# Four sums for the seven-for-eight products: from two engines to one

## The chip, the cores and the metric

One core of a Trainium2 chip runs the kernel. The metric is the device time of one execution in microseconds, the median of several runs.

## The reference

```python
X = np.fft.fft(x, axis=1)                    # x: 8 batches, 3008 rows, 256 columns, float32
X = np.fft.fft(X, axis=2)
x2 = X.real.reshape(24064, 256)
h = x2 @ w_in                                # 256 -> 2048
g = h * (1.0 / (1.0 + np.exp(-1.702 * h)))   # the GELU with a sigmoid
out = g @ w_out                              # 2048 -> 256
```

## The kernel before

The Fourier transforms are matrix products with tables. The rows of a batch are folded first (sums and differences of mirrored columns and rows, `fold1`), then mixed by TensorE (`mix1`, stage one), sent through DRAM (`spill`, `fill`) and mixed again (`stage2`). The column transform is folded into the first weight matrix (`wcs`), so the hidden layer is made straight from stage two's output `pq`.

The second half is a list of 384 steps, `steps`: eight batches, each of three blocks, two halves and eight pairs of hidden chunks, so that a batch has 48 steps. A step `t` makes two chunks of the hidden layer for up to 256 rows and for the mirrored 256 rows. The words "place p" mean the step's number within its batch, `t` modulo 48. Eight steps are a group: they add up in PSUM to one piece of the output.

The output product of two chunks is a product of 2 x 2 blocks. From step 8 on it is done in the manner of Strassen and Winograd, with seven products of blocks in place of eight. That needs four sums of the hidden blocks: S1 = A21 + A22, S2 = S1 - A11, S3 = A11 - A21 and S4 = A12 - S2. For all but the last group (`deep`) three of the products are themselves divided in this way, which needs four more sums for each pair of steps (`deeper`). All blocks stand in one SBUF tile, `big`: A11, A21, S3, S2 of four steps in the part LEFT, and A12, S4, A22, S1 of six steps in the part RIGHT.

The order on every engine is the order in which the code is written (a manual schedule); the engines meet only at semaphores. One iteration `t` of the loop over steps does, for TensorE, the hidden product of step t and the start of step t+1 (`begin`), the output products of step t-3 (`product`, LAG is 3) and the small products of the steps before. For the other engines it does this:

- ACT: `forward(t)`, the GELU of the forward half (L607, from PSUM tile `x` into `big`); `doubled(t+1)`, twice the hidden value (L604, tile `g`); `activate_back(t)`, the GELU of the mirrored half (L614); `middle(t+2)`, which writes the middle term into the PSUM bank of step t+2 (L592). That bank is the one that step t has used, so it must have been read by then. TensorE adds the hidden product of step t+2 to it.
- VectorE: `backward(t)`, which makes the mirrored half from `g` and `x` (L565; it reads the PSUM bank of step t for the last time); then S2 and S4 for a pair of steps (L629, L630; 512 columns in one operation, in every second iteration); then `deeper`, three operations in one iteration and one in the next (L651).
- GpSimd: S1 and S3 of step t (L622 and L623, 256 columns each, in every step), right after `activate_back(t)`.

At the end of a group VectorE also combines the result (`combine`: L757, L758; `combine_small`: L786; `combine_last`: L768, L804) and transposes it (`turn_last`: L737), and around stage two it transposes the new `pq` (L371). In two groups of each batch the second half has 226 rows only; for those `combine` has GpSimd clear a strip of the output buffer (the memset, L752).

Side work is hung on the iterations by `at(t, ...)`, after everything else of the iteration. For the batch after the present one these are, with t0 the first step of the present batch:

```python
for c in range(NCH):                          # 8
    for part in range(2):
        at(t0 + 6 + 2 * c + part + late, fold1, b + 1, c, part, nc.gpsimd)
    if c % 2:
        k = t0 + 9 + 2 * c + late + (c == (5 if late else 1))
        at(k, mix1, b + 1, c // 2)
...
            for k in range(4):
                at(t0 + 31 + 2 * k + late, paced, t0 + 31 + 2 * k + late)
                at(t0 + 31 + 2 * k + late, load_x, b + 2, k)
```

`late` is 5 in the first batch and 0 in the others. So half a fold stands in each of 16 iterations, from place 6 to place 21, in GpSimd's queue between the sums of one step and those of the next: L218 to L220 once for the edge tile `e`, and then for each c L225 and L227 (part 0), L230 and L231 (part 1). All of them read and write SBUF. The rows that they fold were loaded in the batch before, by `load_x` at places 31 to 37 (36 to 42 in the first batch); its DMAs are issued by SP, and a tiny DMA ahead of each (`paced`) holds SP's queue until ACT has reached that step. A fold waits for the load; `mix1` waits for the folds.

Of the kernel before, what the change touches and what calls it, by code (L numbers as in the profile page):

```python
# [29 lines left out]
ALU = mybir.AluOpType  # L30
# [20 lines left out]
def free(ap, offset, *dims):  # L51
    return bass.AP(ap.tensor, ap.offset + offset, [list(ap.ap[0])] + [list(d) for d in dims])
# [60 lines left out]
def kernel(ctx: ExitStack, tc, x, w_in, w_out, tab1, tab2, out):  # L113
    nc = tc.nc
# [12 lines left out]
    op = ctx.enter_context(tc.tile_pool(name="op", bufs=2, space=SB))  # L127
# [25 lines left out]
    big = cv.tile([128, 19 * 1024], F32, tag="big", name="big")  # L153
# [220 lines left out]
    def nyquist(b, blk):  # L374

        nb = nbt[b, blk] = pqp.tile([128, 512], F32, tag="nb", name="nb")
        row = pqt[b, blk][0:1, 1, :]
        if (b, blk) != (0, 0):
            nc.sync.dma_start(out=nb[:], in_=view(Nd, (b * NBLK + blk) * 512, [0, 128], [1, 512]))
            return  # L380
        ps = bank("psn")
        halves(ps[:], ones[:], row, start=True, stop=True)
        nc.scalar.copy(nb[:], ps[:])
# [29 lines left out]
    def squares(key, eng, lo=0, n=1024):  # L413
        g, hi = pre[key][0][:, lo:lo + n], raw[key][:, lo:lo + n, 1].bitcast(F32)
        if eng is nc.scalar:
            eng.activation(g[:], hi, ACTF.Square)
        else:
            eng.tensor_tensor(g[:], hi, hi, op=ALU.mult)
# [5 lines left out]
    def low_up(key, lo=0, n=1024):  # L424

        nc.scalar.activation(pre[key][2][:, lo:lo + n].bitcast(F32), raw[key][:, lo:lo + n, 0], ACTF.Copy, scale=2.0 ** -29,
                             bias=2.0 ** 23)
# [76 lines left out]
    def no_row(c0):  # L504
        nc.sync.dma_start(out=wcs[1][0:1, c0:c0 + 1024], in_=tab1[127:128, n0 + 4:n0 + 1028])

    NP = NF // 2
    steps = [(b, blk, hh, p) for b in range(B) for blk in range(NBLK) for hh in range(2) for p in range(NP)]
    vb, ht, xb, gt, pot = {}, {}, {}, {}, {}
    LEFT, MADE, RIGHT, SUM, RES, OUT = 0, 4096, 8192, 14336, 16384, 18432  # L510
    A11, A21, S3, S2 = range(4)
    A12, S4, A22, S1 = range(4)
# [3 lines left out]
    def width(t):  # L516

        return 226 if steps[t][1:3] == (0, 1) else 256
# [9 lines left out]
    def hidden(t):  # L528

        n = width(t)  # L530
        pa, pb = (bank(name, f"b{i}" if t == NP - 3 else None) for i, name in enumerate(("pa", "pb")))
        for ps, cs in ((pa, 0), (pb, 1)):
            for i in range(2):
                halves(ps[:, i * 256:i * 256 + n], *operands(t, cs, i), start=(i == 0), stop=(i == 1))
        v = sp.tile([128, 512], F32, tag="v", name="v")
        nc.scalar.copy(two(v[:], n), two(pa[:], n))
        vb[t] = v, pa, pb

    def at_left(t, q):
        return LEFT + t % 4 * 1024 + q * 256  # L540

    def at_right(t, q):
        return RIGHT + (t // 2 % 3 * 2 + t % 2) * 1024 + q * 256

    def left(t, q, n):
        return big[:, at_left(t, q):at_left(t, q) + n]

    def right(t, q, n):
        return big[:, at_right(t, q):at_right(t, q) + n]
# [35 lines left out]
    def middle(t):  # L585

        b, blk, hh, p = steps[t]
        n = width(t)
        x = xb[t] = bank("x", f"b{t % 2}")
        for i in range(2):  # L590
            f = 2 * p + i
            nc.scalar.activation(x[:, i * 256:i * 256 + n], nbt[b, blk][:, hh * 256:hh * 256 + n], ACTF.Copy,  # L592
                                 scale=af1[:, f:f + 1])

    def begin(t, cs=0):

        n = width(t)
        for i in range(2):
            halves(xb[t][:, i * 256:i * 256 + n], *operands(t, cs, i), start=False, stop=(cs == 1))
# [13 lines left out]
    def activate_back(t):  # L613
        nc.scalar.activation(back(t), back(t), ACTF.Gelu_apprx_sigmoid)  # L614

    def sums(t, eng):

        if not NP <= t < len(steps):
            return
        n = width(t)  # L620
        if eng is nc.gpsimd:
            eng.tensor_tensor(right(t, S1, n), left(t, A21, n), right(t, A22, n), op=ALU.add)  # L622
            eng.tensor_tensor(left(t, S3, n), left(t, A11, n), left(t, A21, n), op=ALU.subtract)  # L623
            return
        if t % 2 == 0:
            return
        a11, s2 = (free(big[:], at_left(t - 1, q), [1024, 2], [1, n]) for q in (A11, S2))
        a12, s4, s1 = (free(big[:], at_right(t - 1, q), [1024, 2], [1, n]) for q in (A12, S4, S1))
        eng.tensor_tensor(s2, s1, a11, op=ALU.subtract)  # L629
        eng.tensor_tensor(s4, a12, s2, op=ALU.subtract)  # L630

    def deep(t):

        return NP <= t < last
# [301 lines left out]
    n = len(steps)  # L936
# [21 lines left out]
    for b in range(B):  # L958
        t0 = b * NBLK * NF
        late = 0 if b else 5  # L960
# [28 lines left out]
    for t in range(n + LAG):  # L989
        if t < NP:  # L990
            if t == NP - 3:
                spare[:] = [tag for tag in spare if tag[0] == "o"] + ["b2"]
            if t == NP - 1:
                middle(NP)
            hidden(t)
            if t == NP - 1:
                begin(NP)
                no_row(1024)
            if t == 0:
                squares(in2, nc.scalar)  # L1000
                nyquist(0, 0)
                low_up(in2)
                low_down(in2)
            if t in rows_at:
                first_row(rows_at[t])
            if t >= LAG and t != LAG + 1:
                product(t - LAG, 0, None)
            if t == LAG:
                product(1, 0, None)
            if t == 5:  # L1010
                bounds(("out", 2))
            if t == 6:
                low_down(("out", 3))
            if t:
                activate(t - 1)
            if t == 3:
                bounds(("in", 3))
            if t == 5:
                bounds(("out", 3), False)
            if t in early:  # L1020
                fold_w(early[t])
            rows(t)
            if t == NP - 1:
                doubled(NP)
                middle(NP + 1)
        else:
            after, special = (any(fn in (mix1, stage2) for fn, _ in extra.get(k, ())) for k in (t - 1, t))
            if t < n:
                begin(t, 1)
            if t == NP:  # L1030
                activate(t - 1)
            if after and t + 1 < n:
                middle(t + 1)
            if t < n:
                forward(t)
            while waiting:
                m, ps = waiting.pop()
                mixed(m, 1, ps)
            opening = (t - LAG) % NP == 0 and t >= NP + LAG
            one, other = (t - LAG, (1, 2, 4, 7)), (t - LAG - 1, (5, 6, 3))  # L1040
            if opening:
                small_products(*other)
            cut = 0 if opening and not after else 3 if after else 2
            product(t - LAG, 0, cut)
            if after:
                small_products(one[0], one[1][:1])
                small_products(other[0], () if opening else other[1][:1])
            if t + 1 < n:
                begin(t + 1)
            if not opening:  # L1050
                small_products(other[0], other[1][after:])
            product(t - LAG, cut, 6 if t - LAG == last else None)
            small_products(one[0], one[1][after:])
            swap(t - LAG - 2)
            if t < n:
                backward(t)
            if t + 1 < n:
                doubled(t + 1)
            if t < n:
                activate_back(t)  # L1060
                sums(t, nc.gpsimd)
            if t + 2 < n and not special:
                middle(t + 2)
            combine_small(t - LAG - 1)
            if t - LAG == last:
                product(last, 6, None)
            sums(t - 1, nc.vector)
            deeper(t - 2, 0)
            deeper(t - 3, 1)
        if t == NP:  # L1070
            psu.close()
            low = ctx.enter_context(tc.tile_pool(name="low", bufs=1, space=PS))
            pot["low"] = low.tile([128, 3 * 512], F32, tag="low", name="low")
        if t >= LAG:
            combine(t - LAG)
            combine_last(t - LAG - 2)
            turn_last(t - LAG - 3, 0)
            turn_last(t - LAG - 4, 1)
        if t >= NP:
            spare[:] = [f"b{t % 2}"] * special + ["b2"]  # L1080
        for fn, args in extra.get(t, ()):
            fn(*args)
# [28 lines left out]
```

## Time and profile before

| what | value |
|---|---|
| median of 3 runs | 1856.31 us (1854.34 to 1856.57) |
| span of the profiled execution, first to last instruction | 1853.1 us |
| TensorE busy | 1836.6 us |
| VectorE busy | 1520.9 us |
| ACT busy | 1150.5 us |
| GpSimd busy | 975.2 us |
| granted TensorE clock | 0.999 of full speed |

The profiled execution is recorded by its span alone; what lies around it is taken as the difference to the median, 3.2 us. The engines are named PE (TensorE's products), PEld (its weight loads), DVE (VectorE), ACT (ScalarE), POOL (GpSimd) and SP (SyncE, which issues DMAs here). In the timeline a row has its start, its duration, the engine, the line of the kernel, the operation, the tile written and those read, the shapes, how many were merged into the row, and in brackets the idle time before it with what ended it. In a table of waits a row has the total in us, how often, and the longest. In a table of windows a row has the stretch, its length, then for PE, PEld, DVE, ACT and POOL the busy time (and the number of instructions), the granted clock, the share of the DMA engines and GB/s.

### The profile page before, as it was taken

To read this page: it belongs to the slowest core of one execution; us is meant where nothing else is said; L and a number is where in the kernel's file an instruction comes from. 1 tells how busy PE (TensorE), PEld (TensorE's weight loads), DVE (VectorE), ACT (ScalarE), POOL (GpSimd) and SP (SyncE) were. 2 spreads that over 40 slices of the span, in tenths; PEclk is the share of its full clock that TensorE was granted. 3 is DMA by queue.
4 is the path that set the end of the run, shared out by engine and by line. 5 is a ranking of instruction groups with operands and counts; after the bars stand their busy time and mean duration, and the time that the engine had idled before them with its cause. 6 is when DMAs were issued, how large, how long until landed. Compare 5 with 4: busy or idle time off the path is not lost.

```text
span 1853.1 us, 56093 instructions
## 1 busy us (share of the span) xinstructions
PE 1836.6 (99%) x23722; PEld 1401.3 (76%) x23722; DVE 1520.9 (82%) x2222; ACT 1150.5 (62%) x2241; POOL 975.2 (53%) x1053
## 2 busy tenths in 40 slices
PE   8999999999999999999999999999999999999998
PEld 4677777777777777777777777777777777778776
DVE  6988778887798778987789878888888888878874
ACT  5666656665666666666566666666665666656663
POOL 4776446744368434773348643485445754444442
PEclk9999999999999999999999999999999999999999
DMA  8721340215012240223302132121411111100111
GB/s 280 181 61 34 85 67 19 72 52 99 19 46 48 73 81 13 52 50 90 57 13 67 43 86 52 19 75 35 103 31 23 37 46 36 31 19 13 23 19 24
DMA packets 149707, 105.31 MB, mean 57 GB/s; under 512 B 106057, under 2 KB 130665, under 8 KB 148896
## 3 DMA queue, kind: packets, MB, share of 16 engines
q1 hardware_dynamic: 146624, 99.68, 23.6%
q8 instruction: 187, 3.06, 0.7%
q10 hardware_dynamic: 2832, 2.05, 0.5%
q14 instruction: 64, 0.52, 0.1%
HBM read 64.41 MB, written 48.05 MB: 61 GB/s over the span
## 4 chain that ended last, share of the span: by engine, by line
PE 80%; DVE 9%; POOL 4%; ACT 2%; DMA 2%; issue 2%; SPq 0%; DVEq 0%; ACTq 0%; POOLq 0%
PE x L184 29%; PE o L184 22%; PE low L685 21%; PE o L685 3%; DVE big L651 3%; PE ps L255 2%; DVE big L786 2%; DVE big L565 1%; PE ps L365 1%; POOL xt L227 1%; DVE big L629 1%; POOL big L623 1%; DMA xt<-in_x_dram 1%; ACT big L607 1%; DMA Td<-big 1%
## 5 line engine op out<-in xcount | busy, mean ns | idle before, releaser
L622 POOL TENSOR_TENSOR big<-big 128x256 f32<-128x256 f32 (+1 forms) x376 | 353.0, 939 | 825.1 <-ACT big L614 691.4
L184 PE MATMUL x<-pq,wcs 128*64 128x256 f32 (+1 forms) x6016 | 768.8, 376 | 2.0 <-ACT g L604 1.4
L651 DVE TENSOR_TENSOR big<-big 128x512 f32<-128x512 f32 (+1 forms) x736 | 623.1, 861 | 23.4 <-PE low L685 4.7
L184 PE MATMUL o<-big,wo 128*64 128x256 f32 (+1 forms) x4800 | 620.8, 375 | 0.1
L184 PEld LDWEIGHTS x<-pq,wcs 128*64 128x64 f32 x6016 | 412.3, 137 | 186.0 <-issue 15.0
L184 PEld LDWEIGHTS o<-big,wo 128*64 128x64 f32 x4800 | 341.6, 137 | 148.0 <-DVE big L629 0.5
L604 ACT ACTIVATE g<-x 128x512 f32<-128x512 f32 (+1 forms) x376 | 221.6, 589 | 366.3 <-PE x L184 365.0
L565 DVE TENSOR_TENSOR big<-g,x 128x512 f32<-128x512 f32 (+2 forms) x440 | 254.1, 589 | 209.4 <-ACT big L607 209.0
L592 ACT ACTIVATE x<-nb,af 128x256 f32<-128x256 f32 (+1 forms) x752 | 352.9, 469 | 79.7 <-DVE pq L371 63.6
L685 PE MATMUL low<-big 128*64 128x128 f32 (+1 forms) x5888 | 382.8, 270 | 0.0
L685 PEld LDWEIGHTS low<-big 128*64 128x64 f32 x5888 | 337.5, 137 | 29.2
L623 POOL TENSOR_TENSOR big<-big 128x256 f32<-128x256 f32 (+1 forms) x376 | 352.6, 938 | 0.0
L607 ACT ACTIVATE big<-x 128x512 f32<-128x512 f32 (+1 forms) x376 | 219.2, 583 | 127.5 <-PE x L184 121.3
L614 ACT ACTIVATE big<-big 128x512 f32<-128x512 f32 (+1 forms) x376 | 231.9, 617 | 46.0 <-DVE big L565 44.0
L685 PE MATMUL low<-big,wo 128*64 128x128 f32 (+1 forms) x2944 | 220.4, 271 | 0.1
L685 PEld LDWEIGHTS low<-big,wo 128*64 128x64 f32 x2944 | 171.3, 137 | 4.2 <-DVE big L651 1.4
L630 DVE TENSOR_TENSOR big<-big 128x512 f32<-128x512 f32 (+1 forms) x188 | 160.8, 855 | 6.5
L629 DVE TENSOR_TENSOR big<-big 128x512 f32<-128x512 f32 (+1 forms) x188 | 137.3, 730 | 5.3 <-POOL big L622 5.3
L786 DVE TENSOR_TENSOR big<-big,low 128x512 f32<-128x512 f32 (+3 forms) x184 | 109.0, 609 | 3.5
L685 PEld LDWEIGHTS o<-big,wo 128*64 128x64 f32 x1472 | 92.2, 137 | 25.0
L685 PE MATMUL o<-big,wo 128*64 128x128 f32 (+1 forms) x1472 | 110.0, 270 | 0.0
L227 POOL TENSOR_TENSOR xt<-xt 111x510 f32<-111x510 f32 x56 | 86.0, 1535 | 4.4
(95 smaller groups left out, 966.2 us busy)
## 6 DMA issues: line engine op xcount, KB each, us to landing
out_dram<-os SPq DMA_DIRECT2D x284, 64.0 KB
t<-Td SPq DMA_DIRECT2D x22, 512.0 KB
Td<-xt SPq DMA_DIRECT2D x56, 192.0 KB
xt<-in_x_dram SPq DMA_DIRECT2D x14, 512.0 KB
xt<-Xr SPq DMA_DIRECT2D x14, 512.0 KB
nb<-Nd SPq DMA_DIRECT2D x23, 256.0 KB
out_dram<-os SPq DMA_DIRECT2D x96, 56.0 KB
Xr<-in_x_dram SPq DMA_DIRECT2D x7, 752.0 KB
```

The costliest lines, as they stand in the source:

```text
L184: nc.tensor.matmul(out[c0:c0 + 64], lhsT=lhs[:, c0:c0 + 64], rhs=rhs, skip_group_check=True, **how)
L565: nc.vector.tensor_tensor(free(out, at + m - 1, [by, 2], [RUN, blocks], [-1, m]), *ins, op=op)
L592: nc.scalar.activation(x[:, i * 256:i * 256 + n], nbt[b, blk][:, hh * 256:hh * 256 + n], ACTF.Copy, scale=af1[:, f:f + 1])
L604: nc.scalar.activation(two(g[:], n), two(xb[t][:], n), ACTF.Copy, scale=2.0)
L607: nc.scalar.activation(front(t), two(xb[t][:], width(t)), ACTF.Gelu_apprx_sigmoid)
L614: nc.scalar.activation(back(t), back(t), ACTF.Gelu_apprx_sigmoid)
L622: eng.tensor_tensor(right(t, S1, n), left(t, A21, n), right(t, A22, n), op=ALU.add)
L623: eng.tensor_tensor(left(t, S3, n), left(t, A11, n), left(t, A21, n), op=ALU.subtract)
L629: eng.tensor_tensor(s2, s1, a11, op=ALU.subtract)
L630: eng.tensor_tensor(s4, a12, s2, op=ALU.subtract)
L651: nc.vector.tensor_tensor(out, i0, i1, op=how)
L685: nc.tensor.matmul(o, lhsT=lhs, rhs=rhs, start=first_in, stop=(p == NP - 2), skip_group_check=True)
```

## The change

S1 and S3 leave GpSimd. VectorE makes them like S2, for two steps in one operation of 512 columns: in every second iteration it does S1, S3 and S2 of the pair that the two iterations before have finished, in this order. S4 is made one iteration later than the others (in the last group, which needs it sooner, in the same one), ahead of the next three sums of `deeper`. GpSimd keeps, in the loop over steps, the folds of x and the memset. The place of the folds in the code is the same.

```diff
-    def sums(t, eng):
-
-        if not NP <= t < len(steps):
+    def sums(t, part):
+
+        if not NP <= t < len(steps) or t % 2 == 0:
             return
         n = width(t)
-        if eng is nc.gpsimd:
-            eng.tensor_tensor(right(t, S1, n), left(t, A21, n), right(t, A22, n), op=ALU.add)
-            eng.tensor_tensor(left(t, S3, n), left(t, A11, n), left(t, A21, n), op=ALU.subtract)
-            return
-        if t % 2 == 0:
-            return
-        a11, s2 = (free(big[:], at_left(t - 1, q), [1024, 2], [1, n]) for q in (A11, S2))
-        a12, s4, s1 = (free(big[:], at_right(t - 1, q), [1024, 2], [1, n]) for q in (A12, S4, S1))
-        eng.tensor_tensor(s2, s1, a11, op=ALU.subtract)
-        eng.tensor_tensor(s4, a12, s2, op=ALU.subtract)
+        a11, a21, s3, s2 = (free(big[:], at_left(t - 1, q), [1024, 2], [1, n]) for q in range(4))
+        a12, s4, a22, s1 = (free(big[:], at_right(t - 1, q), [1024, 2], [1, n]) for q in range(4))
+        for out, i0, i1, how in (((s1, a21, a22, ALU.add), (s3, a11, a21, ALU.subtract), (s2, s1, a11, ALU.subtract)),
+                                 ((s4, a12, s2, ALU.subtract),))[part]:
+            nc.vector.tensor_tensor(out, i0, i1, op=how)
...
                 activate_back(t)
-                sums(t, nc.gpsimd)
             if t + 2 < n and not special:
                 middle(t + 2)
...
-            sums(t - 1, nc.vector)
+            sums(t - 1, 0)
+            late = t - 2 if deep(t - 2) else t - 1
+            sums(late, 1)
             deeper(t - 2, 0)
             deeper(t - 3, 1)
```

## The prediction

> **What bounds the kernel now.** I read the page's busy row first, then the table of waits, then the timeline of VectorE in two stretches.
>
> ```profile
> PE 1836.6 (99%) x23722; PEld 1401.3 (76%) x23722; DVE 1520.9 (82%) x2222; ACT 1150.5 (62%) x2241; POOL 975.2 (53%) x1053
> ```
>
> TensorE is busy for 1836.6 of 1853.1 us. The table of waits of TensorE between 60 and 1840 us shows how little is left inside:
>
> ```profile
> PE ps L255 <- DVE big L565: 2.5, 5, 0.5
> PE x L184 <- ACT g L604: 1.4, 6, 0.2
> PE x L184 <- ACT x L592: 0.4, 2, 0.2
> ```
>
> The sum is 4.3 us. A faster second engine can win that and hardly more; a slower one can cost much. The Trainium skill (Perfetto Trace Analysis, Identifying the Most-Contended Engine) judges TensorE's headroom not by matmul busy time but by weight loads and by useful work; by it the 76% of PEld would leave up to 24% of 1853.1, some 445 us (an estimate), to be won. The waits above speak against that here.
>
> The whole table of waits says who is early today:
>
> ```profile
> POOL big L622 <- ACT big L614: 691.4, 291, 5.3
> DVE big L565 <- ACT big L607: 209.0, 180, 3.4
> DVE big L629 <- POOL big L622: 5.3, 8, 1.5
> ```
>
> GpSimd stands idle ahead of its sums, which delay VectorE's S2 for 5.3 us only. VectorE is ahead in 180 of the 376 steps (L565 waits for ACT). So the sums' latency is on no path; their place in GpSimd's queue is what matters, and the port they share.
>
> VectorE's operations with two SBUF operands are held up by GpSimd. The timeline of VectorE in a stretch where GpSimd is busy 16.30 of 16.46 us:
>
> ```profile
> 106.90 2.74 DVE L651 TENSOR_TENSOR big<-big 128x452 f32<-128x452 f32 x3
> 111.57 1.09 DVE L629 TENSOR_TENSOR big<-big 128x452 f32<-128x452 f32 x1 [0.75 <-POOL big L622]
> 112.69 0.63 DVE L630 TENSOR_TENSOR big<-big 128x452 f32<-128x452 f32 x1
> 113.24 1.71 DVE L651 TENSOR_TENSOR big<-big 128x452 f32<-128x452 f32 x1
> 115.47 3.29 DVE L651 TENSOR_TENSOR big<-big 128x452 f32<-128x452 f32 x3
> 119.32 1.08 DVE L629 TENSOR_TENSOR big<-big 128x452 f32<-128x452 f32 x1
> 120.43 0.63 DVE L630 TENSOR_TENSOR big<-big 128x452 f32<-128x452 f32 x1
> 120.98 2.38 DVE L651 TENSOR_TENSOR big<-big 128x452 f32<-128x452 f32 x1
> ```
>
> Twelve operations take 13.55 us, 1.13 each. Away from GpSimd the same kind at 512 columns goes at 0.6 to 0.7:
>
> ```profile
> 691.51 2.08 DVE L651 TENSOR_TENSOR big<-big 128x512 f32<-128x512 f32 x3
> ```
>
>  L565, with one operand in PSUM, stays at 641 to 690 ns for 512 columns wherever GpSimd works.
>
> The last view is the end of a group (steps at places 43 to 47 of a batch of 48; p is the step modulo 48), without folds:
>
> ```profile
> 705.19 0.68 DVE L565 TENSOR_TENSOR big<-g,x 128x512 f32<-128x512 f32 x1
> 710.45 0.68 DVE L565 TENSOR_TENSOR big<-g,x 128x512 f32<-128x512 f32 x1
> 711.16 0.63 ACT L614 ACTIVATE big<-big 128x512 f32<-128x512 f32 x1 [0.97 <-DVE big L565]
> 711.70 0.97 ACT L592 ACTIVATE x<-nb,af 128x256 f32<-128x256 f32 x2
> 712.78 1.03 PE L184 MATMUL x<-pq,wcs 128*64 128x256 f32 x8
> ```
>
> These are p=44 and 45. Their forward GELUs (L607) ended at 703.69 and 708.46, so L565 runs 1.5 and 2.0 us late. Behind it ACT does L614 and L592, and TensorE takes that bank at 712.78, 0.11 after L592's end. So TensorE forgives a lateness of about 2.1 us (2.0 + 0.1; by p=44, 1.5 + 0.67 before the matmul at 708.45) and pays everything beyond.
>
> **The change part by part.** *Removed from GpSimd*: 376 L622 and 376 L623, 705.7 us busy, none on the path: 0, but for the queue (below).
>
> *Added to VectorE*: S1 and S3 per pair, 2 x 188 operations at 0.60 clean: 226 us. S4 moves one step later, beside the deeper sums, so each step has four two-operand operations instead of two and four by turns. The delays that go: L651 608 x (857-686) and 128 x (876-622) ns, 136 us; L629, L630 and L768 by the same reckoning some 60; a part stays with the folds. VectorE ends near 1521 + 226 - 120 = 1630 us, 88%: still under TensorE. Outside the folds the group end gets lighter: p=44 now takes 0.6 (L565) + 1.85 + 0.6 + 0.68 (L768) + 0.9 (L804) = 4.6 us where 5.26 stand today (705.19 to 710.45). Worth 0 there, since TensorE loses nothing.
>
> *Moved without being named*: the folds of x. Today two sums of each step stand between the half-folds in GpSimd's queue and wait for that step's ACT, so one half-fold runs per step (places 6 to 21). With the sums gone nothing in that queue waits for a step, but for the memset L752 of the narrow group, which stands behind the folds of c=0 to 5 and waits for the previous use of its buffer at place 14. So the folds run as soon as the load of x lands. That is a batch earlier and without a pause:
>
> ```profile
> 684.00:685.00 1.00, 1.00 (x12) 0.64 (x10) 0.82 (x2) 0.15 (x1) 0.09 (x1) 1.00 1.13 140
> 686.00:687.00 1.00, 1.00 (x24) 1.00 (x22) 0.80 (x2) 0.39 (x1) 0.53 (x1) 1.00 0.00 0
> ```
>
> The last two columns (share of the DMA engines, GB/s) drop to 0 after the load issued at 679.55: it lands near 685.5, at p=40, and the same at 461, 910, 1135 and 1360 us. From there GpSimd has e (0.72 + 0.59 + 0.72) and six folds of 0.20 + 1.27 + 0.71 + 0.72 (the shortest durations of L225, L227, L230, L231): 2.0 + 17.4 = 19.4 us of its own time, straight through p=40 to 44, into the end of the group.
>
> Cost of one such burst: sixteen two-operand operations of VectorE in p=40 to 43, at 1.15 each (1.13 above is for 452 columns). From L565 of p=40 at 684.18: 0.6 + 4 x 1.15 = 689.4; the transposes L371 1.44, 690.8; p=41 from 690.9 by ACT: 0.6 + 4.6, 696.1; p=42: 0.6 + 4.6 + 0.95 (L757, L758), 702.25; p=43: 0.6 + 2.4 (four L786, operand in PSUM) + 4.6, 709.85. L565 of p=44 then runs 709.85 - 703.69 = 6.2 late where 2.16 are forgiven: TensorE loses 4.0 us. After that the folds are through and VectorE (3.2 to 4.6 us a step against 4.7) catches up.
>
> The Trainium skill (SBUF — State Buffer, Who interferes with whom) has such a VectorE operation and a GpSimd one that reads SBUF shut each other out for the whole instruction, whichever starts first. By it alone the 19.4 us less the 7.2 in which VectorE runs L565, L371, L757, L758 and L786 would be waited for in full, 12.2 over sixteen operations, 1.36 each: 7.4 us a burst (an estimate). The trace agrees in kind (1.13 beside busy folds, 0.69 away from them) but not in full size, and I take the row.
>
> Bounds of the unknown price: 0.6 per operation (GpSimd always yields; row 691.51), no loss; 1.30 (113.24 to 123.36, seven operations in 9.09), 6.4.
>
> Other bursts: the second batch's load is issued at 245.7 and lands at 252, p=43 to 44, where the group end is already 1.5 late: 4.5 us, between 0 and 7. The first batch's x is long there, its burst starts near 89 when GpSimd's L481 end; four operations at 1.13 and 0.65 make 5.2 us against steps of 4.2, some 4 to 5 steps, less the 2.1 forgiven: 2.5 us, between 0 and 5. Folds 6 and 7 run at p=14 to 16: 5.8 us of own time, in steps of 4 to 6 us and with the group end over: 0.
>
> Gained: the folds leave p=11 and 12, where L565 comes 2.5 late today and TensorE loses 0.5 five times (L255 above): at most the 4.3.
>
> Sum: 5 x 4.0 + 4.5 + 2.5 - 4.3 = +22.7 on the profiled 1853.1, so 1875.8. The median is 3.2 above that span; I predict 1856.3 + 22.7 = 1879.0. About 0.2%, 3.7 us, can be told from no change.
>
> **The rivals.** *The bursts are absorbed* (faster or equal). Place: L565 of p=44. If it starts by 705.86, TensorE loses nothing; that needs 16 operations in 14.4 us, 0.90 each or less. Then only the gain is left: 1856.3 - 4.3 = 1852.0, with part of it 1854 to 1856. For: L630 at 0.63 in the midst of busy GpSimd; 130 to 160 us run today with VectorE 97% busy and TensorE losing 0.4. Against: 1.13 was measured with two waits of GpSimd for ACT in it.
>
> *GpSimd runs on past a waiting VectorE.* L651 at 120.98 sits out L227's rest and two operations, 2.38 us; the longest is 3132 ns. If that is the rule in an unbroken queue, 1.30 or more each: 5 x 6.4 + 7 + 5 = +44, 1900.
>
> *The folds do not run ahead* (a wait that the order does not show). Then they stay near p=6 to 21 with two more VectorE operations a pair, in steps where VectorE has nothing to spare: each of 7 batches loses 0 to 2 us, 1856 to 1870.
>
> **How the numbers follow.** Forecast 0.60, absorbed 0.22 (faster 0.14, within 0.2% 0.08), running on 0.11, not ahead 0.07 (half within 0.2%). Faster 0.14, same 0.12, slower 0.74. The range goes from the absorbed case with all its gain, 1852, to 1900.
>
> **What would show it.** Right: fold rows of GpSimd at 686 to 710 and not at 760 to 830; VectorE's two-operand rows near 0.6 outside and 1.1 to 1.3 inside; TensorE gaps before x L184 behind ACT L592 at the bursts' ends, 3 to 5 us each; no gap at L255. Wrong: folds one per step, or bursts without a gap.

## The result, and the profile after

The changed kernel takes 1882.05 us (median of 4 runs, 1881.58 to 1884.09) beside 1855.7 for the kernel before (a fourth run has joined the three of the table above): 1.0146 times, 95% interval 1.0131 to 1.016. It is slower by 26 us; the prediction was 1879.0, in a range of 1852 to 1900.

The page after, its busy row, and then the table of waits of TensorE between 60 and 1860 us:

```profile
PE 1842.2 (98%) x23722; PEld 1405.7 (75%) x23722; DVE 1612.3 (86%) x2598; ACT 1148.1 (61%) x2241; POOL 284.8 (15%) x301
```

```profile
PE o L184 <- DVE big L625: 15.0, 8, 2.7
PE low L680 <- DVE big L646: 7.5, 5, 1.6
PE x L184 <- ACT x L592: 2.5, 2, 2.2
PE x L184 <- ACT g L604: 1.4, 6, 0.2
PE o L184 <- POOL xt L225: 0.6, 1, 0.6
```

VectorE has 91 us more work and GpSimd 690 us less, but TensorE, which waited 4.3 us in this part of the run, now waits 27.0. The wait at L255 has gone. The new waits are few and long: eight for L625 (S1, S3, S2, S4 of the pairs) and five for L646 (`deeper`). They are not spread over the run. The timeline of GpSimd shows what stands beside them; these are rows from one of the bursts, the third:

```profile
473.97 0.37 POOL L225 TENSOR_TENSOR xt<-xt 111x4 f32<-111x4 f32 x1 [23.91 <-DMA out_dram<-os]
474.42 1.58 POOL L227 TENSOR_TENSOR xt<-xt 111x510 f32<-111x510 f32 x1
...
495.60 1.05 POOL L230 TENSOR_TENSOR xt<-xt 111x254 f32<-111x254 f32 x1
496.62 1.17 POOL L231 TENSOR_TENSOR xt<-xt 111x254 f32<-111x254 f32 x1
```

Six folds stand one behind the other from 473.97 to 497.79, where before one half stood in each step, at places 6 to 21. (The bracket names the DMA that landed last; the last loads of x had been issued at 467.10 and 467.49.) VectorE in the same stretch:

```profile
473.59 2.96 DVE L625 TENSOR_TENSOR big<-big 128x512 f32<-128x512 f32 x3
476.48 1.21 DVE L646 TENSOR_TENSOR big<-big 128x512 f32<-128x512 f32 x1
480.63 1.18 DVE L625 TENSOR_TENSOR big<-big 128x512 f32<-128x512 f32 x1
481.85 3.50 DVE L646 TENSOR_TENSOR big<-big 128x512 f32<-128x512 f32 x3
485.87 2.96 DVE L625 TENSOR_TENSOR big<-big 128x512 f32<-128x512 f32 x3
488.76 1.21 DVE L646 TENSOR_TENSOR big<-big 128x512 f32<-128x512 f32 x1
493.71 0.68 DVE L625 TENSOR_TENSOR big<-big 128x512 f32<-128x512 f32 x1
494.43 3.91 DVE L646 TENSOR_TENSOR big<-big 128x512 f32<-128x512 f32 x3
498.26 0.68 DVE L565 TENSOR_TENSOR big<-g,x 128x512 f32<-128x512 f32 x1
498.85 1.88 DVE L625 TENSOR_TENSOR big<-big 128x512 f32<-128x512 f32 x3
```

Sixteen two-operand operations take 17.61 us, 1.10 each. The three behind them, after GpSimd has stopped, take 1.88, 0.63 each. And TensorE in two rows of its own timeline:

```profile
490.02 0.66 PE L680 MATMUL low<-big,wo 128*64 128x128 f32 x8 [1.63 <-DVE big L646]
500.79 0.65 PE L184 MATMUL o<-big,wo 128*64 128x256 f32 x4 [1.90 <-DVE big L625]
```

The first waits for the last sum of `deeper` (L646, from 488.76), the second for S2, the last of the three from 498.85. Comparing the start of TensorE's first hidden product (L184, tile x) of every step in both traces gives the loss by places; a place is here the step whose product starts late. Of the 29.2 us between the two profiled spans, 1.6 arise before step 8, where the two kernels do the same; 5.2 at steps 13 to 16, the first burst; 8.8 at steps 46 to 49, the second; 3.97 (1.85 at place 44, 2.12 at 46) in each of the next four and 3.3 in the last; 0.3 at the end; and 5.9 are won back in small pieces, mostly 0.6 to 0.8 at place 14 and 0.2 at place 12 of five batches, and 1.1 at steps 20 to 25 of the first.

Not all of the loss in the first two bursts is waiting. These rows of the second burst are from TensorE's timeline and from the table of windows:

```profile
266.91 1.12 PE L184 MATMUL o<-big,wo 128*64 128x256 f32 x4 [2.69 <-DVE big L625]
267.82 1.92 PE L184 MATMUL x<-pq,wcs 128*64 128x256 f32 x8
268.00:269.00 1.00, 1.00 (x8) 0.53 (x6) 1.00 (x1) 0.00 (x0) 0.92 (x2) 0.50 0.07 16
```

Behind the wait of 2.69 us the granted clock is 0.80, 0.50, 0.50, 0.50 and 0.99 in the five windows of 1 us from 266 us on, that is, one half for some 3.4 us, and eight products for `x` take 1.92 us in place of 1.03. The same follows the wait of 2.48 us at 280 us and that of 2.20 us at 106 us, in the first burst. Three such stretches, up to 1.7 us each (half of 3.4), are some 5 us of the 29.2 (an estimate from their length). In the five later bursts, whose waits are 1.90 us or less, the clock stays at 1.00.

### The profile page after: what moved, and what is told of

Its sections match the earlier page's. It is cut to its first block, busy times and chain, and to the rows that moved or that the text cites. A ratio compares the mean times of both kernels' runs of the same rounds, so it can differ in the third digit from the quotient of the medians.

```text
span 1882.3 us, 55157 instructions
## 1 busy us (share of the span) xinstructions
PE 1842.2 (98%) x23722; PEld 1405.7 (75%) x23722; DVE 1612.3 (86%) x2598; ACT 1148.1 (61%) x2241; POOL 284.8 (15%) x301
## 3 DMA queue, kind: packets, MB, share of 16 engines
q10 hardware_dynamic: 2832, 2.05, 0.5%
## 4 chain that ended last, share of the span: by engine, by line
PE 83%; DVE 9%; POOL 3%; ACT 2%; DMA 2%; issue 1%; ACTq 0%; DVEq 0%; SPq 0%; POOLq 0%
PE x L184 31%; PE o L184 23%; PE low L680 23%; PE o L680 4%; DVE big L646 3%; DVE big L625 3%; PE ps L255 2%; PE ps L365 1%; DVE big L565 1%; DMA xt<-in_x_dram 1%; POOL wo L481 1%; DVE big L781 1%; POOL xt L227 1%; ACT big L607 0%; ACT x L592 0%
## 5 line engine op out<-in xcount | busy, mean ns | idle before, releaser
L184 PE MATMUL x<-pq,wcs 128*64 128x256 f32 (+1 forms) x6016 | 770.8, 377 | 3.9 <-ACT x L592 2.5
L184 PE MATMUL o<-big,wo 128*64 128x256 f32 (+1 forms) x4800 | 624.1, 376 | 15.7 <-DVE big L625 15.0
L184 PEld LDWEIGHTS x<-pq,wcs 128*64 128x64 f32 x6016 | 415.5, 137 | 185.7 <-issue 16.9
L646 DVE TENSOR_TENSOR big<-big 128x512 f32<-128x512 f32 (+1 forms) x736 | 517.7, 724 | 22.6 <-PE low L680 0.2
L625 DVE TENSOR_TENSOR big<-big 128x512 f32<-128x512 f32 (+1 forms) x752 | 505.5, 713 | 0.8 <-ACT big L614 0.7
L604 ACT ACTIVATE g<-x 128x512 f32<-128x512 f32 (+1 forms) x376 | 221.9, 590 | 408.4 <-PE x L184 407.2
L184 PEld LDWEIGHTS o<-big,wo 128*64 128x64 f32 x4800 | 341.2, 137 | 166.5 <-DVE big L625 19.2
L565 DVE TENSOR_TENSOR big<-g,x 128x512 f32<-128x512 f32 (+2 forms) x440 | 256.4, 595 | 173.8 <-ACT big L607 173.1
L592 ACT ACTIVATE x<-nb,af 128x256 f32<-128x256 f32 (+1 forms) x752 | 353.2, 470 | 78.3 <-DVE pq L371 43.7
L607 ACT ACTIVATE big<-x 128x512 f32<-128x512 f32 (+1 forms) x376 | 219.7, 584 | 125.8 <-PE x L184 119.8
L614 ACT ACTIVATE big<-big 128x512 f32<-128x512 f32 (+1 forms) x376 | 231.5, 616 | 34.2 <-DVE big L565 33.2
L218 POOL TENSOR_TENSOR e<-xt 47x254 f32<-47x254 f32 x7 | 6.4, 921 | 546.8 <-DMA xt<-Xr 461.7
L732 DVE STREAM_TRANSPOSE os<-big 128x512 f32<-128x512 f32 x94 | 66.4, 706 | 0.2
```

What stands on the lines that cost most here:

```text
L184: nc.tensor.matmul(out[c0:c0 + 64], lhsT=lhs[:, c0:c0 + 64], rhs=rhs, skip_group_check=True, **how)
L565: nc.vector.tensor_tensor(free(out, at + m - 1, [by, 2], [RUN, blocks], [-1, m]), *ins, op=op)
L604: nc.scalar.activation(two(g[:], n), two(xb[t][:], n), ACTF.Copy, scale=2.0)
L607: nc.scalar.activation(front(t), two(xb[t][:], width(t)), ACTF.Gelu_apprx_sigmoid)
L625: nc.vector.tensor_tensor(out, i0, i1, op=how)
L646: nc.vector.tensor_tensor(out, i0, i1, op=how)
```

## The experiments

The theory: the loss comes from the folds of x, which GpSimd's sums had held to one half per step, and which now run in one burst beside VectorE's two-operand operations. Rival 1: VectorE's added work itself. Rival 2: the later place of S4.

**The folds held back again.** GpSimd does one tiny copy per step where its sums stood:

```diff
+    def tick(t):
+        if NP <= t < len(steps):
+            nc.gpsimd.tensor_copy(beat[:], left(t, A21, 1)[0:1, :])
...
                 activate_back(t)
+                tick(t)
```

> The changed kernel, and in each step GpSimd copies one element of A21 to a scratch tile, at the place where its two sums stood. The copy waits for ACT's mirrored GELU of that step, so the folds are again held to one half per step, at places 6 to 21. Theory (the loss comes from the folds running ahead in one burst): the waits of TensorE for L625 and L646 at places 44 and 46 go, and the time falls from 1882 to 1850 to 1858, at or below the kernel before. Rival 1 (the loss comes from VectorE's 226 us of added work itself): 1870 to 1882, since VectorE's work is that of the changed kernel. Rival 2 (it is S4's later place): 1882 too.

Measured: 1868.72 us, 1.0068 times before (1.0055 to 1.008). Half of the loss goes, half stays, so neither theory nor rival is right alone. The bursts' waits at places 44 and 46 are gone, as expected. What stays lies in two places: 5.5 us at steps 14 to 24 of the first batch, and 1.1 to 1.2 at place 16 of each of the next six. The waits:

```profile
PE o L185 <- DVE big L626: 9.1, 9, 2.5
PE ps L256 <- DVE big L566: 3.1, 7, 0.5
```

(L626 is L625 here, L256 is L255, L566 is L565.) The folds at places 11 to 15 stand in a group's end, and VectorE with two more operations per pair has no time for both there; this is read from where the waits stand, and the copy, which takes 0.2 to 0.6 us of GpSimd in each step, was not tried apart from the folds. Of the 5.5 us in the first batch some 1.7 are the clock: it is halved for 3.4 us behind a wait of 2.47 us. In a run below (the light places) the folds of the first batch stand in the same steps and the wait is 2.46 us, but the clock stays at 1.00, and the 1.67 us that the paced kernel loses at step 15 is not lost.

**No folds at all.** They are left out of the changed kernel:

```diff
-                    at(t0 + 6 + 2 * c + part + late, fold1, b + 1, c, part, nc.gpsimd)
+                    if c == part == 0:
+                        at(t0 + 6 + late, edge_only, b + 1)
```

> The changed kernel with the folds of x left out (the edge tile is cleared by VectorE instead), so GpSimd has nothing to do in the loop over steps but the memsets; the transform is then of unfolded rows. Theory: VectorE's operations of two SBUF operands all take 0.6 to 0.7 us and TensorE has no wait left but those for ACT; 1849 to 1853. Rival 1 (added work of VectorE): 1870 or more. It bounds what any placing of the folds can reach with these sums.

Measured: 1849.88 us, 0.9968 (0.9956 to 0.998), the only case of all four sums on VectorE that is faster than before. The table of VectorE's groups by form, and the waits of TensorE (L650 is L646 here, L629 is L625, L608 is L604 and L596 is L592):

```profile
L650 DVE TENSOR_TENSOR big<-big 128x512 f32<-128x512 f32 x608 | 406.2, 689 | 18.5
L629 DVE TENSOR_TENSOR big<-big 128x512 f32<-128x512 f32 x624 | 401.1, 684 | 0.8 <-ACT big L618 0.7
```

```profile
PE x L184 <- ACT g L608: 1.1, 6, 0.2
PE x L184 <- ACT x L596: 0.3, 1, 0.3
```

With the same VectorE work as in the slow kernel, nothing waits for VectorE. So rival 1 is out as it stands: the added work costs nothing where no fold runs beside it. It is the two together that cost. (Without the folds the result is not the transform; the run is for its time alone.)

**S3 alone.** S1 stays with GpSimd, in each step:

```diff
+                first_sum(t)          # GpSimd: S1 = A21 + A22 of step t
...
-        for out, i0, i1, how in (((s1, a21, a22, ALU.add), (s3, a11, a21, ALU.subtract), (s2, s1, a11, ALU.subtract)),
+        for out, i0, i1, how in (((s3, a11, a21, ALU.subtract), (s2, s1, a11, ALU.subtract)),
```

> Half of the change: S3 goes to VectorE as in the changed kernel, and S4 to its later place, but S1 stays with GpSimd, 256 columns in each step (so it also holds the folds to one half per step). VectorE has 113 us more work than before instead of 226. Theory: the folds do not run ahead, so no burst and no loss, 1851 to 1859. Rival 1 (in proportion to VectorE's added work): half of the loss, 1866 to 1871. Rival 2 (S4's later place): 1882.

Measured: 1855.38 us, 0.9998 (0.9989 to 1.0007), no change. One sum of the two on VectorE, with the folds still held to the steps, is free in sum: 0.8 us at most is lost at a single place, and as much is won at others. S4 has its later place here too, so rival 2 is out.

**A longer burst.** The memset that stops GpSimd's queue behind the sixth fold goes to VectorE:

```diff
-            nc.gpsimd.memset(oc[:, :, n:], 0.0)
+            nc.vector.memset(oc[:, :, n:], 0.0)
```

> The changed kernel with the memset L747 on VectorE, so that nothing holds folds 6 and 7 back: all eight run in the burst, 5.8 us more of GpSimd's own time through places 44 to 46, and none at places 14 to 16. Theory: each of the six later bursts costs 2 to 4 us more, 1892 to 1904. Rivals 1 and 2 (the burst does not matter): 1880 to 1883.

Measured: 1899.86 us, 1.0241 (1.0227 to 1.0255), 17.8 us over the changed kernel's 1882.05. By the two traces the second burst costs no more than before, and the five later ones 2.4 to 3.5 more each. The third costs 1.85 + 3.93 + 1.67 at places 44, 46 and 47 where it cost 1.85 + 2.12. A longer burst costs more, as the theory has it, but by two ways: TensorE's wait for S2 at place 46 grows from 1.90 to 3.71 us, and behind it the granted clock is one half for 3.4 us, which is the 1.67 at place 47. Four of the five later bursts have such a stretch here; none had one in the changed kernel.

**S2 ahead of S3.** To see which wait comes last:

```diff
-        ... (s1, a21, a22, ALU.add), (s3, a11, a21, ALU.subtract), (s2, s1, a11, ALU.subtract)
+        ... (s1, a21, a22, ALU.add), (s2, s1, a11, ALU.subtract), (s3, a11, a21, ALU.subtract)
```

> The changed kernel with S2 ahead of S3 in VectorE's order (S1, S2, S3), everything else the same. It tells which wait of TensorE comes last at place 46. If S2 ends last (the product's second operand, as its wait for L625 says), S2 is some 0.5 us earlier and each of the six later bursts and the first lose that much less: 1877 to 1880. If the chain L565, L614, L592 of my prediction ends last: 1881.5 to 1882.5.

Measured: 1878.59 us, 1.013 (1.0117 to 1.0144), 3.5 us less than the changed kernel. At place 46 a burst now costs 1.63 in place of 2.12. The waits of TensorE:

```profile
PE o L184 <- DVE big L625: 10.4, 8, 1.8
PE low L680 <- DVE big L646: 8.6, 5, 1.9
PE x L184 <- ACT x L592: 4.4, 3, 2.2
```

The wait for L625 falls from 15.0 to 10.4 and that for ACT's L592 grows from 2.5 to 4.4: S2 came last where the wait shrank, and the chain L565, L614, L592 is close behind. But the 3.5 us are not the 0.5 per burst of the expectation, though they fall into its range. In the three bursts from the fourth to the sixth the 0.5 won at place 46 is lost again at places 44 (0.24) and 47 (0.19). Of the 5.8 us between the two profiled spans, 3.0 lie in the second burst, where TensorE's two longest waits are 1.97 and 1.82 us in place of 2.69 and 2.48 and the granted clock stays at 1.00; 1.1 lie in the first burst, and 1.7 before step 8, where the kernels are the same. So it is shown for place 46 that S2 came last there, and not that its place in the order is worth 3.5 us.

**Other places for the folds.** If folds cost where VectorE has no time, they might be put where it has. Three kernels put the half folds of the later batches at sixteen places, some of them twice:

```diff
+    light = -1, 0, 0, 1, 1, 2, 7, 8, 8, 9, 9, 10, 15, 16, 17, 18
...
-                    at(t0 + 6 + 2 * c + part + late, fold1, b + 1, c, part, nc.gpsimd)
+                    at(t0 + light[2 * c + part] if b else 11 + 2 * c + part, fold1, b + 1, c, part, nc.gpsimd)
```

With the paced kernel's sums:

> The paced kernel (one-element copy in each step), with the half folds of the later batches moved from places 6 to 21 to sixteen places where VectorE waits for ACT: -1, 0, 0, 1, 1, 2, 7, 8, 8, 9, 9, 10, 15, 16, 17, 18; the first batch keeps its places 11 to 26. Theory (what costs is a fold beside two-operand operations of VectorE in steps with no time to spare, wherever it stands): the 1.2 us at place 16 of six batches go, and the 0.2 and 0.6 us at places 12 and 14 are won as without folds; the first batch keeps its 5.5. 1854 to 1859. Rival (the added work costs by itself): 1866 to 1870, as paced.

Measured: 1882.1 us, 1.0143 (1.0128 to 1.0159): a miss by more than 20 us. With the kernel before's sums:

> The kernel before, all its sums as they were, with the half folds of the later batches at the same sixteen places. It tells what the places are worth without the change. Theory: the 0.5 us waits of TensorE at L255 (place 12) go and no others come, 1851 to 1855. Rival (places do not matter): 1855.5 to 1856.5.

Measured: 1859.99 us, 1.0029 (1.002 to 1.0038): a miss too. With the old sums up to step 31 and the new ones from there:

```diff
+    SWAP = 32
...
+        if NP <= t < SWAP:            # GpSimd: S1 and S3 of step t, as before the change
...
+        elif SWAP <= t < len(steps):  # GpSimd: the one-element copy
```

> As the kernel with the light places, but up to step 31 the sums are made as before the change (S1 and S3 by GpSimd), and from step 32 on by VectorE with the one-element copy. Theory: the first batch's 5.5 us go too; what stays is near the kernel without folds (1849.9): 1850 to 1854, faster than before by 2 to 6. Rival (the added work costs by itself): 1862 to 1866.

Measured: 1878.18 us, 1.0123 (1.0109 to 1.0137): the third miss. The reason is in the choice of places. Four steps had two halves, and those were small bursts: in the first of the three, a batch loses 0.7 and 0.9 at places 2 and 4 and 1.65 at place 12. Even with GpSimd's own sums (the second) 0.93 go at place 7. The first batch, whose sums the third kernel makes in the old way up to step 31, loses nothing from step 11 to its end, where the paced kernel lost 5.5; that part held.

**One half per step.** The same with single places:

```diff
-    light = -1, 0, 0, 1, 1, 2, 7, 8, 8, 9, 9, 10, 15, 16, 17, 18
+    light = -7, -6, -1, 0, 1, 2, 6, 7, 8, 9, 10, 15, 16, 17, 18, 19
```

(The folds of the second and third batch keep their old places, since the condition is now `b > 1`; so it is the fourth to the eighth batch's folds that move, one batch fewer than the text below says.) With the old sums up to step 31, then the new:

> As the kernel with light places and the old sums up to step 31, but never two half folds in one step: places -7, -6, -1, 0, 1, 2, 6, 7, 8, 9, 10, 15, 16, 17, 18, 19 for the third to the eighth batch, 6 to 21 for the second batch after the first. The doubled places lost 5 us per batch. Theory (what counts is GpSimd's own time per step beside VectorE's two-operand operations): with one half per step and none in the group ends nothing is lost and 0.8 us per batch is won: 1850 to 1855. Rival (with all four sums on VectorE any fold beside them costs): 1860 to 1870.

Measured: 1860.99 us, 1.0031 (1.002 to 1.0042). The doubled places' loss is gone, but 1.15 us remain at place 44 of five batches, behind the halves at places 41 and 42, and 1.2 at step 64 (place 16), in the batch whose folds kept their places. It lies between the theory's range and the rival's. With the kernel before's sums throughout:

> The kernel before with all its sums, and the half folds at the same single places. Theory: the waits at L255 go here too, 1851 to 1854; the sums' engine then makes no difference of more than 2 us beside the kernel above. Rival (places do not matter): 1855 to 1856.

Measured: 1851.74 us, 0.9986 (0.9978 to 0.9995), faster than both kernels. The waits of TensorE from 60 to 1830 us:

```profile
PE x L184 <- ACT g L604: 1.4, 6, 0.2
PE ps L255 <- DVE big L565: 0.5, 1, 0.5
PE x L184 <- ACT x L592: 0.2, 1, 0.2
```

The wait at L255 was 2.5 us, five times 0.5; one is left, that of the batch whose folds kept their places. At the same places the sums' engine makes 9 us of difference, to the disadvantage of the change; the theory's "no more than 2" was wrong. So the rival has its share: with one half per step, S1 and S3 were still dearer on VectorE than on GpSimd. The loss is not at every fold, however: 1.15 us at place 44 and 0.2 at place 46, behind the halves at 41 and 42, and 1.2 at step 64; the halves at places -1 to 2, 6 to 10 and 15 to 19 lose nothing. A kernel without the two halves at 41 and 42 was not run.

## Why the prediction was right, point by point

*What binds.* TensorE lost nothing to the sums' latency before; moving them could win 4.3 us at most. The kernel without folds is 6 us faster than before: this held but for a microsecond or two.

*The folds run ahead.* They did, from the landing of x, at place 40, and with the memset as the only halt: folds 7 and 8 stand behind it, in the third batch from 583.21 to 591.15 us, which is places 15 to 17, without loss. The step that carried the forecast was this one, and the longer burst and the paced copy both confirm it.

*The price of a burst.* 1.15 us per operation was taken; 1.10 is measured. A loss of 4.0 was worked out; 3.97 is measured four times and 3.3 once. That the two agree so closely is partly luck, as the next point shows.

*The wait that ends last.* Wrong. I let the loss come at x, behind L565, L614 and L592, when VectorE is over 2.16 us late. It came 1.85 at the last sum of `deeper` and 2.12 at S2. L565 at 498.26 is 3.8 late against L607's end, with 1.9 already lost before it: 5.7 in all where I had 6.2. The sum came out right since the two deadlines are close: ACT's L592 for that step ended at 500.47, and without the wait for S2 TensorE would have stood at x at 501.27 - 1.90 = 499.37, so it would still have lost 1.1.

*The other bursts.* Under-sized both: the second 8.8 for 4.5, the first 5.2 for 2.5. In the second the burst begins when the group end has begun, and takes in L763 at 267.38 (1.75) and L799 at 269.23 (1.29), two-operand operations that my count left out: away from the burst they take 0.68 and 0.96 (501.26 and 502.04). That is 1.4 more of VectorE's time. The larger part is a term that the prediction did not have: the granted clock, one half for 3.4 us behind each of two waits in the second burst and behind one in the first, some 3.4 and 1.7 us of the measured 8.8 and 5.2. Without it 5.4 and 3.5 would be left (an estimate).

*The gain.* 5.9 for 4.3; most of it is the 0.6 to 0.8 at place 14, where the table of waits showed 0.5.

Terms together: 19.2 + 8.8 + 5.2 - 5.9 = 27.3 for 22.7. The errors have both signs, and the clock, some 5.1 us, is about as large as the whole difference; the median moved by 26.4. So the mechanism, bursts of folds beside two-operand operations at the group ends, was right, and the last wait and the clock were not seen.

*VectorE busy* 1612 us for 1630. *The rivals.* "Absorbed" was out by the price of an operation. "Not ahead", 1856 to 1870, is what the paced copy makes, 1868.7: its 0 to 2 us per batch are measured as 1.1 to 1.2, and 5.5 in the first. So had the folds stayed in place, the change would have been slower all the same.

## What to carry to other kernels

An instruction in a queue is also a pace for what stands behind it: before taking it out, look at what it holds back, when that will start instead, and beside what. A share of busy time over the run (86%) hides that: the loss lay in a few steps at the end of groups, where VectorE was 2 us late before. A long wait can cost more than its length, so look at the granted clock behind it too. When work moves between VectorE and GpSimd, count the two-operand operations that meet in the same step, and place background work one piece per step, away from steps that are late already.

## What was not expected of the hardware

With folds beside them, S1 and S3 cost more on VectorE than on GpSimd: with the folds at the same single places, all four sums on VectorE (from step 32 on) took 1861.0 us and two on each engine 1851.7, though VectorE's operations are the faster ones (0.63 us for 512 columns against 0.73 for 256). And the stretch before step 8, the same in all these kernels, differed by up to 4.0 us between their profiled executions and that of the kernel before, so a difference of 2 us between single spans says nothing. (In the two with the most, 4.0 and 2.4 us, the granted clock was halved for 3.4 us near 29 us.)

The halved clock itself was not expected. In the twelve traces, behind 85 us, TensorE has 15 waits of 2.05 us or more; 11 of them are followed by 3.4 us at half of the clock, 4 are not (2.07, 2.18, 2.46 and 2.97 us). Behind shorter waits there is none, apart from the kernel's last microseconds. What decides between the 11 and the 4 was not tested.
